# Two fold weights read in 4096-byte packets: whole rows of w3, pairs of rows of w_out, and a transpose by every second column

## The chip, the cores and the metric

The kernel runs on one core of one Trainium2 chip. The metric is the device time of one execution in microseconds (us); the time before is the median of three runs.

## The reference

Windowed attention with sink tokens, then a multiplicative feed-forward block:

```python
# q, k, v: (4, 8, 768, 64) float32; n_sink = 4, window = 128
scores = q @ k.T / sqrt(64), kept where key < 4 or 0 <= query - key < 128
x = (softmax(scores) @ v), heads side by side            # (3072, 512)
out = (((x @ w1) * (x @ w2)) @ w3) @ w_out               # w1, w2: 512x1024; w3: 1024x1024; w_out: 1024x512
```

All inputs and the output are float32; the kernel works in bfloat16.

## The kernel before

No activation stands between w3 and w_out, so the kernel first makes their product, the *fold* `w3o = w3 @ w_out` (1024 x 512, bfloat16), and then needs one projection for each token instead of two. For the fold, `fold_w3` (L398) transposes each block of 128 rows of w3 on TensorE, four 128 x 128 squares into a PSUM tile (L402), and VectorE copies them out (L407). `fold_mm` (L421) multiplies the eight transposed squares of row block `i` with the eight row blocks of w_out (L432), two at a time, and ScalarE copies the sum to `w3o` (L436, L439). Both weights lie in SBUF as bfloat16 (`w3_sb`, `wo_sb`), with a block of 128 rows for each index of the second dimension and one row in each partition.

The weights come in two ways. *Raw loads* (`load_raw`, L151) are issued by SP at the start: nine transfers of 512 KB of float32 into buffers that are only needed later (`homes`, L147), each then cast to bfloat16 by VectorE (w3) or ScalarE (w_out) (`cast`, L410). Each takes two row blocks, 512 columns wide. The rest of w3 comes through POOL's queue (`load_rows`, L114), which casts on the way, as do k, q and v (L106) and w1 and w2 (L110). The order of POOL's loads is the list `order` (L138), and POOL starts it only when the fifth raw load has landed (`hold`, L136, and the small copy at L195).

After the fold's first part the kernel goes through four batches: for each block of 256 tokens transposes of k and q (L205 on TensorE for the first two batches, by DMA for the others), scores and exponentials (L255, L276), masked, times v (L308, L345), a transpose of the result (L324, L361), then the two gate products with w1 and w2 (L385), their elementwise product, and the projection with `w3o` (L446) and the output's transfer (L453).

The engines' programs are written by hand-made planning at build time: every piece of work is a `task` (L513) with its stages, costs, predecessors and loads; `landings` (L475) forecasts when each load is there; from L724 on a loop always takes the task that can start first, with a priority among equals. The order that comes out is fixed in the program. Where the planner sees a gap on TensorE in the first 40 us, it puts in fillers, `keep_busy` (L456): products of a zero tile, whose result nobody reads. `need` (L524) tells the fold's tasks which cast or which load they wait for; the transposes of a w3 block need its columns, the products need w_out's blocks.

Of the kernel before, what the change touches and what calls it, by code (L numbers as in the profile page):

```python
# [21 lines left out]
def kernel(  # L22
# [13 lines left out]
    nc = tc.nc  # L36
    FP32 = mybir.dt.float32
# [7 lines left out]
    P = 128  # L45
# [3 lines left out]
    DM = H * D  # L49
# [61 lines left out]
        nc.gpsimd.dma_start(out=dst[:, :, n0:n1],  # L111
                            in_=src[:, n0:n1].rearrange("(ko ki) n -> ki ko n", ki=P))

    def load_rows(dst, src, i0, i1, cols):  # L114
        nc.gpsimd.dma_start(out=dst[:, i0:i1, cols],
                            in_=src[i0 * P:i1 * P, cols].rearrange("(ko ki) n -> ki ko n", ki=P))

    def load(what, *i):
        if what == "qkv":
            if i[1] == 0:  # L120
                nc.gpsimd.memset(vN[i[0]][:, :, :, D:D + 1], 1.0)
            for kb in range(i[1], i[2]):
                load_qkv(i[0], kb)
        elif what == "w3":
            load_rows(w3_sb, moe_w3, i[0], i[0] + 2, slice(i[1] * 512, i[2] * 512))
        elif what == "wo":
            load_rows(wo_sb, moe_w_out, i[0], i[1], slice(0, DM))
        else:
            for dst, src in ((w1_sb, moe_w1), (w2_sb, moe_w2)):
                load_w(dst, src, i[0] * 256, i[1] * 256)  # L130


    raws = [("w3", 0, 0, "dve"), ("wo", 0, 0, "act"), ("w3", 2, 0, "dve"), ("wo", 2, 0, "act"),
            ("w3", 4, 0, "dve"), ("wo", 4, 0, "act"), ("w3", 0, 1, "dve"), ("wo", 6, 0, "act"),
            ("w3", 2, 1, "dve")]
    hold = 5  # L136

    order = [("qkv", 0, 0, 1), ("w3", 4, 1, 2), ("qkv", 0, 1, 2), ("w3", 6, 0, 2), ("qkv", 0, 2, 3),  # L138
             ("qkv", 0, 3, 4), ("w12", 0, 1), ("w12", 1, 2), ("w12", 2, 3), ("w12", 3, 4), ("qkv", 0, 4, 5),
             ("qkv", 0, 5, 6), ("qkv", 1, 0, 6), ("qkv", 2, 0, 6), ("qkv", 3, 0, 6)]  # L140

# [2 lines left out]
    def flat(tile_, names):  # L144
        return tile_[:].rearrange(f"p {names} -> p ({names})")
# [2 lines left out]
    homes += [(flat(kN[1], "k s"), 0), (flat(qN[1], "k s"), 0), (flat(kqT[1], "i k s"), 0), (flat(kqT[1], "i k s"), 2048),  # L148
              (flat(xT[1], "k s"), 0), (flat(vN[2], "k h d"), 0)]

    def load_raw(n, what, i, h, act):  # L151
        home, at = homes[n]
        tile_ = home[:, at:at + 2048].bitcast(FP32).rearrange("p (k n) -> p k n", n=512)
        dst, src = (w3_sb, moe_w3) if what == "w3" else (wo_sb, moe_w_out)
        nc.sync.dma_start(out=tile_, in_=src[i * P:(i + 2) * P, h * 512:h * 512 + 512].rearrange(  # L155
            "(ko ki) n -> ki ko n", ki=P))
        return dst[:, i:i + 2, h * 512:h * 512 + 512], tile_

    ctx.enter_context(tc.manual_schedule(engines={
        mybir.EngineType.PE, mybir.EngineType.Activation, mybir.EngineType.DVE, mybir.EngineType.SP,  # L160
# [31 lines left out]
    for b in range(B):  # L192
        nc.gpsimd.tensor_copy(vs[b][:, :, D], ones_s[:])
    if hold:
        nc.gpsimd.tensor_copy(spent[:], casts[hold - 1][1][:, 0, 0:1])  # L195
    for x in order:
        if x[0] != "qkv" or x[1] == 0:
            load(*x)
# [199 lines left out]
    def fold_w3(i, j0, j1):  # L398

        tp = ps_mm.tile([P, j1 - j0, P], BF16, tag="mm", name="tp3")  # L400
        for j in range(j0, j1):
            nc.tensor.transpose(tp[:, j - j0, :], w3_sb[:, i, j * P:(j + 1) * P], ident)  # L402
        yield
        if i not in w3T:
            w3T[i] = (flat((kN, qN)[i - 4][1], "k s")[:, 2048:3072].rearrange("p (k n) -> p k n", n=P)
                      if i in (4, 5) else work.tile([P, KFF, P], BF16, tag="w3t", bufs=4, name="w3t"))
        nc.vector.tensor_copy(w3T[i][:, j0:j1, :], tp[:])  # L407
        yield

    def cast(act, dst, src):  # L410

        (nc.scalar.copy if act else nc.vector.tensor_copy)(dst, src)  # L412
        yield
# [51 lines left out]
    def service(what, *i):  # L465
        if what == "qkv":
            return [(0.95 if i[0] == 0 else 0.87, 0.845 + (1.2 if i[0] in XPOSE and x != "v" else 0.7 if (x, *i) == ("v", 0, 4, 5) else 0.0), [(x, i[0], kb)])
                    for kb in range(i[1], i[2]) for x in "kqv"]
        if what == "w3":
            return [(0.75, 1.3 * (i[2] - i[1]), [("w3", i[0], h) for h in range(i[1], i[2])])]  # L470
        if what == "wo":
            return [(0.81, 0.65 * (i[1] - i[0]), [("wo", x, 0) for x in range(i[0], i[1], 2)])]
# [46 lines left out]
    for n, ((what, i, h, e), ap) in enumerate(zip(raws, casts)):  # L519
        task(("c", what, i, h), n, cast(e == "act", *ap), [(e, 1.04 if e == "act" else 0.69)],  # L520
             loads=[("raw", what, i, h)])
    raw_keys = {x[:3] for x in raws}

    def need(what, i, h):  # L524
        key = (what, i // 2 * 2, h)
        return ([("c",) + key], []) if key in raw_keys else ([], [key])

    for i in range(KFF):
        for h in range(2):
            j0, j1 = 4 * h, 4 * h + 4  # L530
            needs = [need("w3", i, x) for x in range(j0 // 4, j1 // 4)]
            task(("t3", i, h), 100 + i + (5 if i < SPLIT and h else 0), fold_w3(i, j0, j1),
                 [("pe", 0.057 * (j1 - j0)), ("dve", 0.05 + 0.075 * (j1 - j0))],
                 [x for a, _ in needs for x in a], [x for _, a in needs for x in a],
                 started=[("t3", i, 0)] if i >= SPLIT and h else [folded(i - SPLIT)] if i >= SPLIT else [], ring="mm")
        for h, (j0, j1) in enumerate(FM[i]):
            last = j1 == KFF
            begin = i < 4 and i % 2 == 0 and h == 0
# [268 lines left out]
```

## Time and profile before

| | us |
|---|---|
| median of three runs | 198.62 (198.33 to 198.84) |
| profiled execution | 198.11 |
| its span | 196.40 |
| TensorE busy | 189.7 (97% of the span) |
| VectorE busy | 115.0 |
| ScalarE busy | 104.9 |
| GpSimd busy | 76.0 |

The profiled execution's time is 1.7 us longer than its span, which counts from the first to the last recorded instruction. In the rows, PE is TensorE's products, PEld its weight loads, DVE is VectorE, ACT ScalarE, POOL GpSimd, SP SyncE. A row of the timeline gives the start, the length from the first start to the last end, engine, line, operation, tiles and shapes, the number of instructions that follow each other, and in brackets the idle time of the engine ahead of them and what ended it. The names are those of the buffers: `w_sb` stands for all weight tiles, `ab`, `kN`, `qN` and `kqT` also for the buffers that a raw load borrows.

| queue | what | issues, KB each |
|---|---|---|
| SP | raw loads of w3 and w_out (L155) | 9, 512 |
| POOL | w1 and w2 (L111), a part of w3 (L115) | 9 of 256, 1 of 512 (as written) |
| POOL | k, q, v (L108) | 72, 128 (as written) |
| SP | output (L453) | 24 of 25 |

### The profile page before, as it was taken

Reading aid. Unit: us, or ns where it says so; the run is one execution under the profiler, and the core shown is the slowest. Engines: PE = TensorE matmul, PEld = TensorE weight load, DVE = VectorE, ACT = ScalarE, POOL = GpSimd, SP = SyncE. Lnnn points to the kernel's source line nnn. Section 1 sums busy time; section 2 is a strip of 40 time slices with the busy share of each in tenths; the row PEclk is TensorE's granted clock in tenths of the full one; section 3 lists DMA queues with packets and bytes.
Section 4 is the critical chain, followed back from the end, with each engine's and each line's share of the span. In section 5 each row is a group of like instructions: output and inputs, shape, how many; then the busy total and the mean of one; then the engine's idle time right before and its main releaser. Section 6 shows DMA issues by size and latency. Waiting matters only on the chain.

```text
span 196.4 us, 4491 instructions
## 1 busy us (share of the span) xinstructions
PE 189.7 (97%) x1778; PEld 119.2 (61%) x1792; DVE 115.0 (59%) x268; ACT 104.9 (53%) x174; POOL 76.0 (39%) x104
## 2 busy tenths in 40 slices
PE   7999889999999999999999999999999999999994
PEld 2345566988867687666666655666555556654443
DVE  4544778755767878687879738777644034440000
ACT  2334557744825788876777355556653433332332
POOL 5189967689999953745557000000000000000000
PEclk9999999999999999999999999999999999999999
DMA  5999999999999999999999999920232600002334
GB/s 145 390 389 189 184 158 197 196 162 154 156 152 212 187 183 125 153 162 177 158 151 159 121 156 178 97 57 2 53 110 107 180 35 3 0 0 96 143 140 158
DMA packets 105445, 28.35 MB, mean 144 GB/s; under 512 B 95184, under 2 KB 99920, under 8 KB 105424
## 3 DMA queue, kind: packets, MB, share of 16 engines
q0 software_dynamic: 79648, 12.33, 89.7%
q1 hardware_dynamic: 25632, 15.67, 35.7%
q8 instruction: 14, 0.23, 0.4%
q14 instruction: 7, 0.06, 0.1%
q10 hardware_dynamic: 144, 0.07, 0.1%
HBM read 29.36 MB, written 6.29 MB: 182 GB/s over the span
## 4 chain that ended last, share of the span: by engine, by line
PE 85%; DMA 8%; POOL 4%; SPq 1%; issue 1%; DVE 0%; ACT 0%
PE pg L385 43%; PE po L446 21%; PE av L345 7%; PE sc L255 5%; DMA ab<-in_moe_w_dram 4%; DMA w_sb<-in_moe_w_dram 4%; PE tp L205 3%; PE pw L432 2%; POOL qN L108 1%; PE xt L361 1%; POOL vN L108 1%; PE av L308 1%; SPq L155 1%; POOL kN L108 1%; PE sp L237 1%; PE sc L276 1%
## 5 line engine op out<-in xcount | busy, mean ns | idle before, releaser
L385 PE MATMUL pg<-xT,w_sb 128*128 128x384 bf16 (+1 forms) x576 | 90.8, 308 | 0.0
L385 PEld LDWEIGHTS <-w_sb 128*128 128x128 bf16 x576 | 53.5, 98 | 25.4 <-issue 0.5
L389 DVE TENSOR_TENSOR ab<-a_sb,pg 128x384 bf16<-128x384 f32 (+1 forms) x72 | 36.6, 508 | 29.1 <-PE pg L385 24.3
L392 ACT COPY a_sb<-pg 128x384 f32<-128x384 f32 (+1 forms) x72 | 32.0, 444 | 37.2 <-PE pg L385 17.8
L446 PE MATMUL po<-w3o,ab 128*128 128x512 bf16 (+2 forms) x198 | 42.6, 362 | 0.5
L260 ACT ACTIVATE ex<-sc 128x1024 bf16<-128x1024 f32 (+1 forms) x40 | 37.8, 964 | 5.0 <-PE sc L255 4.5
L446 PEld LDWEIGHTS <-ab 128*128 128x128 bf16 x208 | 19.3, 98 | 20.1 <-issue 0.3
L450 ACT COPY w_sb<-po 128x512 f32<-128x512 f32 (+2 forms) x25 | 14.1, 566 | 25.9 <-PE po L446 24.0
L264 DVE TENSOR_TENSOR am<-ex,maskt 128x1024 bf16<-128x1024 bf16 (+1 forms) x40 | 25.4, 645 | 4.0 <-ACT ex L260 4.0
L108 POOL DMA_DIRECT2D vN<-in_v_dram x24 | 21.9, 912 | 12.3 <-DMA kN<-in_k_dram 10.6
L108 POOL DMA_DIRECT2D qN<-in_q_dram x24 | 22.0, 917 | 5.9 <-DMA vN<-in_v_dram 3.8
L108 POOL DMA_DIRECT2D kN<-in_k_dram x24 | 21.7, 906 | 4.4 <-DMA qN<-in_q_dram 2.6
L352 DVE TENSOR_TENSOR xn<-av,rec 128x256 bf16<-128x256 f32 x40 | 17.0, 425 | 1.4
L345 PE MATMUL av<-vN,am 128*128 128x65 bf16 x296 | 16.4, 193 | 0.0
L345 PEld LDWEIGHTS <-am 128*128 128x128 bf16 x296 | 14.3, 97 | 2.4 <-issue 0.2
L349 DVE RECIPROCAL rec<-av 128x4 f32<-128x4 f32 x40 | 7.2, 179 | 11.0 <-PE av L345 10.7
L255 PE MATMUL sc<-kqT 64*128 64x128 bf16 (+1 forms) x216 | 11.6, 238 | 0.0
L345 PE MATMUL av<-vs,es 128*128 128x130 bf16 x56 | 11.0, 221 | 0.1
L207 DVE COPY kqT<-tp 128x1024 bf16<-128x1024 bf16 x12 | 8.3, 690 | 3.8 <-PE tp L205 3.6
L450 DVE COPY w_sb<-po 128x128 f32<-128x128 f32 x1 | 0.3, 292 | 16.3 <-ACT w_sb L450 16.3
L255 PEld LDWEIGHTS <-kqT 64*128 64x128 bf16 x216 | 6.9, 94 | 4.0 <-issue 3.2
L432 PE MATMUL ph<-wo_sb,w3t 128*128 128x512 bf16 x32 | 8.1, 379 | 0.5 <-ACT wo_sb L412 0.4
(71 smaller groups left out, 145.1 us busy)
## 6 DMA issues: line engine op xcount, KB each, us to landing
out_dram<-w_sb SPq DMA_DIRECT2D x23, 256.0 KB, 2.2
kN<-in_k_dram POOLq DMA_DIRECT2D x24, 128.0 KB, 8.0
qN<-in_q_dram POOLq DMA_DIRECT2D x24, 128.0 KB, 8.0
vN<-in_v_dram POOLq DMA_DIRECT2D x24, 128.0 KB, 7.8
w_sb<-in_moe_w_dram POOLq DMA_DIRECT2D x9, 256.0 KB, 8.4
ab<-in_moe_w_dram SPq DMA_DIRECT2D x3, 512.0 KB, 6.1
ab<-in_moe_w_out_dram SPq DMA_DIRECT2D x3, 512.0 KB, 7.0
kN<-in_moe_w_dram SPq DMA_DIRECT2D x1, 512.0 KB, 9.2
```

Of the source, the lines that this page charges most:

```text
L108: nc.gpsimd.dma_start(out=dst, in_=rows(src, b, kb))
L255: nc.tensor.matmul(sc[:, e, c:c + n], kT[b][hp, r, kb * P:(kb + 1) * P], qT[b][hp, r, qb * P:qb * P + n], start=True, stop=True)
L260: nc.scalar.activation(ex[:, :, c0:], sc[:, :, c0:], ACTF.Exp, scale=scale)
L264: nc.vector.tensor_mul(am[:, :, c0:], ex[:, :, c0:], mk)
L345: nc.tensor.matmul(o, lhs, rhs, start=(n == 0), stop=(n == len(todo) - 1), skip_group_check=True)
L352: nc.vector.tensor_mul(xns[b, t][:, :, r, :, :], av[:, :, :, 0:D], rec[:].to_broadcast([P, 2, 2, D]))
L385: nc.tensor.matmul(pg[:], w_sb[:, kk, dt * P:(dt + 1) * P], xT[b][:, kk, tk], start=(kk == 0), stop=(kk == NP - 1))
L389: nc.vector.tensor_mul(ab[b][:, dt, tk], gate_a.pop((b, c, dt))[:], pg[:])
L392: nc.scalar.copy(a_sb[:], pg[:])
L432: nc.tensor.matmul(po, w3T[i][:, j, :], wo_sb[:, j, :], start=(j == 0), stop=(j == KFF - 1))
L446: nc.tensor.matmul(po[:], ab[b][:, kk, m * P:(m + 1) * P], w3o[:, kk, n0:n1], start=(kk == 0), stop=(kk == KFF - 1))
L450: (nc.vector.tensor_copy if n0 == DM // 2 else nc.scalar.copy)(o_sb, po[:])
```

## The change

Raw loads and POOL's loads of w3 take whole rows: a raw load of w3 is now one block of 128 rows, 1024 columns wide, so that each partition reads 4096 adjacent bytes where it read two runs of 2048. A raw load of w_out takes 256 rows as before, but partition p gets rows 2p and 2p+1 of them, which lie next to each other, again 4096 bytes. So index j of `wo_sb` no longer holds rows 128j to 128j+127, but every second row of a group of 256. The transposes of w3 follow: square j takes every second column of w3, from j // 2 * 256 + j % 2, so that the products still pair the same rows and columns.

The raw loads' order changes with it: w_out's first 256 rows come first, then w3 and w_out in turn, and the ninth is w3's fifth block. POOL keeps one block of w3 (rows 640 to 767) as its first weight load, where it had the right halves of two blocks, and its last two blocks, which it read by whole rows already. The planner's tables follow the new units; its costs for a raw load, a cast and a transpose are the same numbers.

```diff
-    def load_rows(dst, src, i0, i1, cols):
-        nc.gpsimd.dma_start(out=dst[:, i0:i1, cols],
-                            in_=src[i0 * P:i1 * P, cols].rearrange("(ko ki) n -> ki ko n", ki=P))
+    def fold_rows(what, i0, i1):
+
+        src = (moe_w3 if what == "w3" else moe_w_out)[i0 * P:i1 * P, :]
+        if what == "w3":
+            return src.rearrange("(ko ki) n -> ki ko n", ki=P)
+        return src.rearrange("(g ki ko) n -> ki g (ko n)", ki=P, ko=2)
+
+    def load_rows(dst, what, i0, i1):
+        dst = dst[:, i0:i1, :]
+        if what == "wo":
+            dst = dst.rearrange("p (g ko) n -> p g (ko n)", ko=2)
+        nc.gpsimd.dma_start(out=dst, in_=fold_rows(what, i0, i1))
...
-    raws = [("w3", 0, 0, "dve"), ("wo", 0, 0, "act"), ("w3", 2, 0, "dve"), ("wo", 2, 0, "act"),
-            ("w3", 4, 0, "dve"), ("wo", 4, 0, "act"), ("w3", 0, 1, "dve"), ("wo", 6, 0, "act"),
-            ("w3", 2, 1, "dve")]
+    raws = [("wo", 0, 2, "act"), ("w3", 0, 1, "dve"), ("wo", 2, 4, "act"), ("w3", 1, 2, "dve"),
+            ("wo", 4, 6, "act"), ("w3", 2, 3, "dve"), ("wo", 6, 8, "act"), ("w3", 3, 4, "dve"), ("w3", 4, 5, "dve")]
     hold = 5
...
-    order = [("qkv", 0, 0, 1), ("w3", 4, 1, 2), ("qkv", 0, 1, 2), ("w3", 6, 0, 2), ("qkv", 0, 2, 3),
+    order = [("qkv", 0, 0, 1), ("w3", 5, 6), ("qkv", 0, 1, 2), ("w3", 6, 8), ("qkv", 0, 2, 3),
...
-    def load_raw(n, what, i, h, act):
+    def load_raw(n, what, i0, i1, act):
         home, at = homes[n]
-        tile_ = home[:, at:at + 2048].bitcast(FP32).rearrange("p (k n) -> p k n", n=512)
-        dst, src = (w3_sb, moe_w3) if what == "w3" else (wo_sb, moe_w_out)
-        nc.sync.dma_start(out=tile_, in_=src[i * P:(i + 2) * P, h * 512:h * 512 + 512].rearrange(
-            "(ko ki) n -> ki ko n", ki=P))
-        return dst[:, i:i + 2, h * 512:h * 512 + 512], tile_
+        tile_ = home[:, at:at + 2048].bitcast(FP32)
+        nc.sync.dma_start(out=tile_.rearrange("p (k n) -> p k n", k=1), in_=fold_rows(what, i0, i1))
+        return flat((w3_sb if what == "w3" else wo_sb)[:, i0:i1, :], "k n"), tile_
...
         for j in range(j0, j1):
-            nc.tensor.transpose(tp[:, j - j0, :], w3_sb[:, i, j * P:(j + 1) * P], ident)
+            nc.tensor.transpose(tp[:, j - j0, :], w3_sb[:, i, bass.ds(j // 2 * 256 + j % 2, P, step=2)], ident)
...
         if what == "w3":
-            return [(0.75, 1.3 * (i[2] - i[1]), [("w3", i[0], h) for h in range(i[1], i[2])])]
+            return [(0.75, 1.3 * (i[1] - i[0]), [("w3", x) for x in range(*i)])]
...
-            needs = [need("w3", i, x) for x in range(j0 // 4, j1 // 4)]
+            needs = [need("w3", i)]
...
-            needs = [need("wo", x, 0) for x in range(j0, j1, 2)]
+            needs = [need("wo", x) for x in range(j0, j1)]
```

In the built program TensorE's stream has the same work ahead of the transposes of k and q for the fifth token block of the first batch, and the same order from there on. Ahead of them 19 fillers stand instead of 16, and the fold's pieces stand in the new order of the loads.

More of the change, by code (lines that the diff above doesn't have):

```diff
@@ L124, in load @@
         elif what == "w3":
-            load_rows(w3_sb, moe_w3, i[0], i[0] + 2, slice(i[1] * 512, i[2] * 512))
+            load_rows(w3_sb, what, *i)
         elif what == "wo":
-            load_rows(wo_sb, moe_w_out, i[0], i[1], slice(0, DM))
+            load_rows(wo_sb, what, *i)
         else:
@@ L194 @@
     if hold:
-        nc.gpsimd.tensor_copy(spent[:], casts[hold - 1][1][:, 0, 0:1])
+        nc.gpsimd.tensor_copy(spent[:], casts[hold - 1][1][:, 0:1])
     for x in order:
@@ L469, in service @@
         if what == "w3":
-            return [(0.75, 1.3 * (i[2] - i[1]), [("w3", i[0], h) for h in range(i[1], i[2])])]
+            return [(0.75, 1.3 * (i[1] - i[0]), [("w3", x) for x in range(*i)])]
         if what == "wo":
-            return [(0.81, 0.65 * (i[1] - i[0]), [("wo", x, 0) for x in range(i[0], i[1], 2)])]
+            return [(0.81, 0.65 * (i[1] - i[0]), [("wo", x) for x in range(*i)])]
         return [(0.8, 1.34 * (i[1] - i[0]), [(w,) + (n,) for n in range(i[0], i[1])]) for w in ("w1", "w2")]
@@ L517, in task, with need @@
                            slots=slots, paced=paced)
[L519 to L526, printed above, removed]
+    made = {}
+    for n, ((what, i0, i1, e), ap) in enumerate(zip(raws, casts)):
+        task(("c", what, i0), n, cast(e == "act", *ap), [(e, 1.04 if e == "act" else 0.69)],
+             loads=[("raw", what, i0, i1)])
+        made.update({(what, i): ("c", what, i0) for i in range(i0, i1)})
+    def need(what, i):
+        return ([made[what, i]], []) if (what, i) in made else ([], [(what, i)])
     for i in range(KFF):
```

## Prediction

> **What bounds the kernel now.** I read the page first, then the chain of waits in order of time, then the timeline of the first 36 us, then the order of the instructions in both programs.
>
> ```profile
> span 196.4 us, 4491 instructions
> PE 189.7 (97%) x1778; PEld 119.2 (61%) x1792; DVE 115.0 (59%) x268; ACT 104.9 (53%) x174; POOL 76.0 (39%) x104
> PE 85%; DMA 8%; POOL 4%; SPq 1%; issue 1%; DVE 0%; ACT 0%
> ```
>
> TensorE has the end: 85% of the chain is its own. The next fences are the chain of waits in order of time (start, length, what) and the busy times by stretch (length, then each engine's busy time and instructions, for the first row TensorE's alone; then granted clock, DMA share, GB/s).
>
> ```profile
> 0.81 0.46 SPq L155
> ...
> 2.85 7.84 DMA ab<-in_moe_w_dram
> ...
> 10.74 0.71 POOL spent L195
> ...
> 11.69 0.81 POOL kN L108
> ...
> 18.32 7.46 DMA w_sb<-in_moe_w_dram
> ...
> 25.83 0.41 PE tp L402 x4
> ...
> 28.01 0.45 PE tp L205 x8
> 28.45 0.86 PE pw L432 x4
> ...
> 30.87 0.33 PE sc L276 x8
> ...
> 31.74 0.24 PE av L308 x8
> 31.99 0.22 PE sp L237 x4
> ...
> 33.73 0.36 PE av L308 x10
> ...
> 37.65 2.62 PE pg L385 x24
> ...
> 43.22 0.22 PE tp L205 x4
> ```
>
> ```profile
> 25.83:43.22 17.39, 17.17 (x221) 1.00 1.83 181
> ```
>
> ```profile
> 60.00:100.00 40.00, 39.84 (x476) 27.45 (x476) 31.17 (x80) 31.32 (x51) 25.01 (x30) 1.00 1.95 168
> 100.00:140.00 40.00, 39.95 (x399) 24.89 (x398) 28.99 (x68) 23.11 (x39) 4.37 (x5) 1.00 1.17 106
> ```
>
> The reader is to see two regimes. From 25.83 on TensorE is full, at a granted clock of 1.00, and sets its own pace. Before, the chain runs through transfers: the fifth raw transfer lands (2.85 + 7.84 = 10.69), POOL starts its loads, and the last w3 rows land at 25.78. So time is to be had only where TensorE stands without useful work ahead of some 28 us. The order view says that both programs' TensorE streams are the same from the transposes at 43.22 on, and that ahead of them they hold the same work but for 19 fillers instead of 16. So the change is worth the difference in idle and filler time up to that mark, and that difference stays to the end.
>
> By the chain's rows, a transpose takes 0.45/8 = 0.056 us, a fold product 0.86/4 = 0.215, a gate product of 256 columns 2.62/24 = 0.109. Up to the mark the order view counts 64 fold products (13.8), 112 transposes (6.3) and 64 gate products (7.0) in both programs, seven groups of scores at 0.33 (2.3), three and four groups of values at 0.24 and 0.36 (2.2), and two sink steps, each taken at 0.22 (0.4): 32.0 us of work. Before stands **43.22 - 32.0 = 11.2 us without work**.
>
> **The change part by part.** The timeline's rows for the start (start, length, engine, line, tile):
>
> ```profile
> 1.33 4.87 PE L460 MATMUL pz<-ksbd 128*128 128x512 bf16 x11 [1.33 <-DVE ksbd L165]
> ...
> 5.32 0.79 DVE L412 CAST w_sb<-ab 128x1024 bf16<-128x1024 f32 x1 [1.73 <-DMA ab<-in_moe_w_dram]
> ...
> 6.17 0.78 PE L402 MATMUL tp<-ident,w_sb 128*128 128x128 bf16 x8
> 6.67 1.04 ACT L412 CAST wo_sb<-ab 128x1024 bf16<-128x1024 f32 x1 [4.59 <-DMA ab<-in_moe_w_out_dram]
> ...
> 8.00 0.69 DVE L412 CAST w_sb<-ab 128x1024 bf16<-128x1024 f32 x1 [0.47 <-DMA ab<-in_moe_w_dram]
> ...
> 8.75 0.62 PE L402 MATMUL tp<-ident,w_sb 128*128 128x128 bf16 x8
> ...
> 9.35 1.04 ACT L412 CAST wo_sb<-ab 128x1024 bf16<-128x1024 f32 x1 [1.63 <-DMA ab<-in_moe_w_out_dram]
> ...
> 9.67 2.76 PE L432 MATMUL ph<-wo_sb,w3t 128*128 128x512 bf16 x12
> ...
> 25.00 0.39 PE L460 MATMUL pz<-ksbd 128*128 128x512 bf16 x1
> 25.83 0.40 PE L402 MATMUL tp<-ident,w_sb 128*128 128x128 bf16 x4 [0.45 <-DMA w_sb<-in_moe_w_dram]
> ```
>
> *Raw transfers.* Each moves 512 KB before and after; the casts show one landing every (9.35 - 5.32)/3 = 1.34 us. What changes is 128 packets of 4096 bytes for 256 of 2048. No HWDGE packet of 4096 bytes reading HBM is in this trace. The nearest rows are the raws themselves (queue totals of 6 to 14 us) and the POOL load of the last w3 rows, which already reads whole rows (22.5 to 23.5 us; packets counted at the 2048 bytes written, so twice that is read):
>
> ```profile
> DMA packets 1620, 3.12 MB, mean 390 GB/s; under 512 B 96, under 2 KB 96, under 8 KB 1620
> q1 hardware_dynamic: 1620, 3.12, 104.8%
> ```
>
> ```profile
> q0 software_dynamic: 97, 0.20, 104.9%
> ```
>
> At the same share of the engines 390 GB/s stand against 97 x 4096 bytes in 1 us, 397, or 400 by the rounded megabytes. Bounds: no gain (1.34 us a raw), and a tenth (1.21), which no row here reaches. I take 1.29, a little over the nearest row, as its packets are also cast: 0.05 us a raw, 0.2 at the fourth landing, 0.45 at the ninth.
>
> The Trainium skill (DMA: Bandwidth & Descriptors, "Why small descriptors are slow (HBM only)") gives each packet about 3 cycles on top of its 32-byte beats; as an estimate from that page 3/67 at 2048 bytes becomes 3/131 at 4096, 2.2% saved, a raw of 1.31 and a sum 0.2 us poorer than below (nine raws at 0.02 ahead of the last load). The POOL row's 2% agrees with it.
>
> *Order of the raws and start of the fold.* w_out comes first, so the first w3 rows are the second landing: 6.67 - 0.1 = 6.57, cast 0.79, hop 0.06 (8.00 + 0.69 to 8.75), transposes at 7.4, where 6.17 stood before. The four added fillers cover it: ten spacings in 4.87 less a last one of 0.57 are 0.43 each, so twelve to fifteen end between 7.3 and 7.8, and either hides in the next wait. The second w3 block needs the fourth landing: 9.35 - 0.2 + 0.69 + 0.06 = **9.90**. TensorE has done eight transposes and four products by then (1.3 us), since only w_out's first blocks are there: 8.6 without work. The gap between transposes and their products (copy by DVE) is 9.67 - 8.75 - 0.45 = 0.47; the new order has it twice more (it puts one filler in each): 9.5. From about 15 us on, all of w_out and four w3 blocks are there and the order finds work for every copy.
>
> *The last loads.* POOL's hold is on the fifth landing, 0.25 earlier; its first load was issued at 11.69, yet between 6 and 14 us the raws' queue alone moved (the only queue row above), so I let its stream begin as the raws end, 0.45 earlier; the load of w3 rows 640 to 767 has 128 packets instead of 256. The last w3 rows land some 0.5 earlier, 25.3. Counted as above, 15.4 us of work stand ahead of their transposes before (so 25.83 - 15.4 = 10.4 without work there); the new order has the same work and four more transposes there, 15.6. TensorE comes to them at 15.6 + 9.5 = 25.1 and the load ends at 25.3: the filler and most of the wait of 25.00 to 25.83 go, and 25.3 - 15.6 = 9.7 are without work. After that, before loses another 11.2 - 10.4 = 0.8; the new order puts twelve transposes in a row ahead of one pair of products, so I add a half gap, 0.25. **After: 9.7 + 1.05 = 10.75 without work, 0.5 less than before.**
>
> *Transposes by every second column.* 64 weight loads now read w3_sb with a step of two elements.
>
> ```profile
> L402 PEld LDWEIGHTS <-w_sb x64: 95/98/152, 6.2 to 27.3; 128*128 128x128 bf16 x64
> ```
>
> ```profile
> 79.24 0.71 PE av L345 x20
> ```
>
> Twenty matmuls with a load each take 0.71, so a load with adjacent elements holds TensorE at most 36 ns, though its record lasts 98. A transpose takes 56. No load with a step is in this trace: its cost is bounded by 0 (it hides under the 56) and by the whole record exposed, 98 - 56 = 42 ns. I take 0, by the 20 ns of slack of the nearest row.
>
> The Trainium skill (TensorE: Matmul & The Clock Gate, "Weight-path perf modes — Fast Weight Load (FWL) and DoubleRow") speaks against this: the fast load reads 32 bits at a time, two bf16, and a step of two leaves one of use. As an estimate a load would then hold 72 ns, 16 more than a transpose, 0.8 us for the 48 transposes that don't stand in a wait, and the sum would be +0.3. The same table allows a step, and no run here shows one.
>
> *Nothing* I count for the rest: five casts of 0.69 on DVE, four of 1.04 on ACT, sixteen copies of 0.42 and nine SP issues stay, and POOL's order is the same. The products pair w3 and w_out rows of the same index, so their sum is unchanged.
>
> **Sum:** 196.4 - 0.5 = 195.9 of span. The profiled execution took 198.11, 1.7 over its span: 197.6. It lies 0.5 under the median of 198.62, so on that scale 198.1.
>
> **The rivals.**
>
> *The step costs (slower).* The loads stand in front of every transpose; the first 16 fall into waits for landings, 48 are on the path after 10 us. At 42 ns each 2.0 us go, with -0.5 that is +1.5: **200.1**. From 10 ns a transpose on (66 ns instead of 56) the gain is gone; from 23 ns on the kernel is slower by over 0.3%. For it: no such load is known here. Against: the 20 ns of slack.
>
> *The ramp shrinks too (faster).* The first landing comes at 5.32, 4.5 us after its issue at 0.81, against 1.34 between the later ones. If a part of that start goes by packet, half as many packets bring every landing some 0.5 more forward, the POOL stream with them: **197.6**. Against: bytes may set it, not packets.
>
> *The last load holds.* If POOL's stream doesn't come forward, the last w3 rows still land at 25.78 and TensorE waits for them from 25.1 on; 25.8 - 15.6 + 1.05 = 11.25 without work: **198.6**, no change. For it: the chain passes through this very load; in POOL's order six loads of k, q and v stand ahead of it, which the change leaves alone.
>
> *The new order meets waits that the planner does not see.* It still plans 1.31 us a raw and the old price of a transpose; three more gaps of 0.47 between copies and products in 15 to 25 us, where I count none, cost 1.4: **199.5**.
>
> **How the numbers follow.** The forecast, 197.6 to 198.6, has 0.46; its middle lies close to what a measurement of this kernel can just tell from no change, 0.3% or 0.6 us, so I split it 0.23 faster, 0.23 same. The ramp 0.15 (faster), the last load 0.10 (same), the step 0.23 (slower), new waits 0.06 (slower). Faster 0.38, same 0.33, slower 0.29. The range goes from 197.2, beyond the ramp's case by what a raw of 1.21 would add in the first four landings, to 200.1, which takes in a step at 42 ns.
>
> **What would show it.** Casts about 1.29 apart (a raw's gain right) or 1.34 (wrong); eight transposes of L402's successor in 0.45 (no cost of the step) or 0.6 and more; first transposes at 7.4, second block at 9.9; no wait of a transpose on a w_sb load at 25 to 26 us; the transposes of 43.22 at about 42.7. If these stand at 43.2 or later while the casts came closer, the time went to waits between 10 and 28 us; if the stream after the mark is longer, my claim that the difference stays is wrong.

## The result, and the profile after

The kernel after takes **197.92 us** (median of 22 runs, 196.73 to 198.6), the kernel before 198.53 on the same chip (22 runs, 198.06 to 199.82). The ratio is 0.996, with a 95% interval from 0.9946 to 0.9975: 0.6 us or 0.4% faster. The profiled execution took 197.96 us, 1.7 over its span.

The page, head and chain by engine:

```profile
span 196.3 us, 4494 instructions
PE 188.9 (96%) x1781; PEld 118.8 (61%) x1795; DVE 114.6 (58%) x268; ACT 105.2 (54%) x174; POOL 75.4 (38%) x104
PE 86%; DMA 7%; DVE 3%; issue 1%; ACT 1%; SPq 1%; POOL 0%
```

The span is 0.1 shorter than that of before, although the median fell by 0.6; the profiled execution of before (198.11) lies 0.4 under its own median, that of after at its median. So the two spans are not the gain; the places where the streams part are what the traces can show.

The timeline of the start (casts, then TensorE's transposes of the first two w3 blocks):

```profile
4.19 1.04 ACT L418 CAST wo_sb<-ab 128x1024 bf16<-128x1024 f32 x1 [2.10 <-DMA ab<-in_moe_w_out_dram]
5.43 0.69 DVE L418 CAST w_sb<-ab 128x1024 bf16<-128x1024 f32 x1 [1.84 <-DMA ab<-in_moe_w_dram]
7.53 1.04 ACT L418 CAST wo_sb<-ab 128x1024 bf16<-128x1024 f32 x1 [2.29 <-DMA ab<-in_moe_w_out_dram]
8.80 0.69 DVE L418 CAST w_sb<-ab 128x1024 bf16<-128x1024 f32 x1 [1.42 <-DMA ab<-in_moe_w_dram]
10.09 1.04 ACT L418 CAST wo_sb<-ab 128x1024 bf16<-128x1024 f32 x1 [1.51 <-DMA ab<-in_moe_w_out_dram]
11.37 0.70 DVE L418 CAST w_sb<-ab 128x1024 bf16<-128x1024 f32 x1 [0.63 <-DMA ab<-in_moe_w_dram]
...
6.19 0.62 PE L408 MATMUL tp<-ident,w_sb 128*128 128x128 bf16 x8
...
8.63 0.59 PE L438 MATMUL ph<-wo_sb,w3t 128*128 128x512 bf16 x2 [0.92 <-ACT wo_sb L418]
...
9.55 0.62 PE L408 MATMUL tp<-ident,w_sb 128*128 128x128 bf16 x8
```

From the third landing on a raw transfer lands every (11.37 - 7.53)/3 = 1.28 us, where it was 1.35. The first landing comes 1.1 us earlier than before, but between the second and the third lie 2.1 us, so that the fourth is only 0.55 ahead (8.80 for 9.35). The queue totals between 6 and 14 us agree in direction, 401 GB/s for 390:

```profile
DMA packets 1103, 3.21 MB, mean 401 GB/s; under 512 B 327, under 2 KB 327, under 8 KB 1103
q1 hardware_dynamic: 883, 3.18, 98.9%
```

The chain of waits in order of time shows what replaced the w3 load that held TensorE at 25.78:

```profile
2.20 6.58 DMA ab<-in_moe_w_dram
8.80 0.70 DVE w_sb L418
9.55 0.41 PE tp L408 x4
...
42.50 0.45 PE tp L211 x8
...
52.41 6.92 DMA qN<-in_q_dram
59.38 0.40 PE tp L211 x4
```

It now leaves the transfers at the fourth raw landing, 2.20 + 6.58 = 8.78, and passes no load from there to the mark. The mark, 43.22 before, stands at **42.50: 0.72 us earlier**. But at 52 us the chain goes back to a transfer, q of the second batch's fifth token block (of six). The waits of TensorE on other engines and queues between 6 and 70 us (total, times, longest):

```profile
PE ph L438 <- ACT wo_sb L418: 0.9, 1, 0.9
PE pw L438 <- DVE w3t L413: 0.4, 1, 0.4
PE tp L211 <- DMA qN<-in_q_dram: 0.4, 1, 0.4
PE ph L438 <- DVE w3t L413: 0.3, 1, 0.3
```

No wait of a product on w_sb is left in this list, though the second block's transposes still start when their cast ends (8.80 + 0.69 = 9.49); the filler ahead of them covers most of that wait. The third row is the new one; its place in the timeline, and the same transposes in the kernel before:

```profile
58.60 0.40 PE L211 MATMUL tp<-ident,kN 128*128 128x128 bf16 x4
59.38 0.40 PE L211 MATMUL tp<-ident,qN 128*128 128x128 bf16 x4 [0.38 <-DMA qN<-in_q_dram]
```

```profile
59.18 0.38 PE L205 MATMUL tp<-ident,kN 128*128 128x128 bf16 x4
59.53 0.40 PE L205 MATMUL tp<-ident,qN 128*128 128x128 bf16 x4
```

Laid instruction by instruction over that of before, TensorE's stream is 0.89 ahead at 43.4, 0.84 at 49.8, and 0.15 from 59.5 to the last product. In this execution, then, most of what the fold gained went back to POOL's stream of k, q and v. The landings in the two traces show how: from the second batch's first load to v of its third block POOL's loads land 0.7 to 0.8 us earlier than before, nearly as much as TensorE had gained. The next load, k of the fourth block, follows 1.72 us behind that v, where it was 1.15, and from there the stream is less than 0.3 ahead: the q that TensorE waits for lands at 59.33, before at 59.48.

### The profile page after: what moved, and what is told of

The parts are those of the page before. It is cut to its first block, busy times and chain, and to the rows that moved or that the text cites. A ratio compares the mean times of both kernels' runs of the same rounds, so it can differ in the third digit from the quotient of the medians.

```text
span 196.3 us, 4494 instructions
## 1 busy us (share of the span) xinstructions
PE 188.9 (96%) x1781; PEld 118.8 (61%) x1795; DVE 114.6 (58%) x268; ACT 105.2 (54%) x174; POOL 75.4 (38%) x104
## 4 chain that ended last, share of the span: by engine, by line
PE 86%; DMA 7%; DVE 3%; issue 1%; ACT 1%; SPq 1%; POOL 0%
PE pg L391 41%; PE po L452 19%; PE av L351 6%; PE sc L261 5%; DMA qN<-in_q_dram 4%; PE pw L438 3%; DMA ab<-in_moe_w_dram 3%; PE ph L438 3%; PE tp L211 2%; PE tp L408 1%; PE av L314 1%; PE xt L367 1%; PE sc L282 1%; DVE w3t L413 1%; PE sp L243 1%
## 5 line engine op out<-in xcount | busy, mean ns | idle before, releaser
L438 PE MATMUL ph<-wo_sb,w3t 128*128 128x512 bf16 x32 | 8.6, 380 | 1.4 <-ACT wo_sb L418 0.9
```

The lines of the kernel that those rows point to most:

```text
L438: nc.tensor.matmul(po, w3T[i][:, j, :], wo_sb[:, j, :], start=(j == 0), stop=(j == KFF - 1))
```

## The experiments

They ran in four groups, the first two on one chip and the last two on another, each beside the kernels of its group and runs of the kernel before (median 198.69, 199.0, 198.44 and 198.43 in the four). Times are medians, and ratios, to the kernel before of the same group, have their 95% interval behind them.

**Order alone: the packets of 2048 bytes again.** POOL's loads of w3 by whole rows stay as in the kernel after; no run parts them from the order.

```diff
-        nc.sync.dma_start(out=tile_.rearrange("p (k n) -> p k n", k=1), in_=fold_rows(what, i0, i1))
+        if what == "w3":
+            src = moe_w3[i0 // 2 * 256:i0 // 2 * 256 + 256, i0 % 2 * 512:i0 % 2 * 512 + 512]
+        else:
+            src = moe_w_out[i0 * P:i1 * P, :]
+        nc.sync.dma_start(out=tile_.rearrange("p (k n) -> p k n", n=512),
+                          in_=src.rearrange("(ko ki) n -> ki ko n", ki=P))
```

> The changed kernel, but each raw load reads the same bytes in 256 packets of 2048, as before: two row blocks by 512 columns of w3, two rows 128 apart of w_out. Order, sizes, step of the transposes and TensorE's stream stay; the fold pairs wrong rows, so the output is not the reference's. Theory (the packets bring the raws forward): landings again at 5.3 and every 1.34 us, second w3 block's transposes at 10.1 instead of 9.55, the mark (transposes of k and q for the fifth token block) at 43.0 to 43.3 instead of 42.5, time within 0.3 us of the kernel before. Rival (the new order of loads and products does it): landings late, but the mark at 42.5 to 42.7 and the changed kernel's time.

198.57 us, 0.9991 (0.9973 to 1.0009): no gain. The casts stand at 4.29, 6.85, 8.58 and 9.94, then 1.35 apart as before, and TensorE's transposes of the second w3 block wait for the fourth of them (timeline, TensorE):

```profile
9.68 0.59 PE L443 MATMUL ph<-wo_sb,w3t 128*128 128x512 bf16 x2 [0.55 <-ACT wo_sb L423]
10.11 0.38 PE L471 MATMUL pz<-ksbd 128*128 128x512 bf16 x1
10.69 0.62 PE L413 MATMUL tp<-ident,w_sb 128*128 128x128 bf16 x8 [0.20 <-DVE w_sb L423]
```

They start at 10.69, 1.1 later than in the kernel after, and the transposes of k for the fifth token block stand at 43.70, later than in the kernel before (the profiled execution was the longest of its runs, 198.97). The new order needs the landings early: it has less to do than the old one until the second block is there. Its first landing at 4.29 also shows that the early start does not come from the larger packets alone.

**Packets alone: the old order and tiling with raw transfers of 4096 bytes.**

```diff
-        nc.sync.dma_start(out=tile_, in_=src[i * P:(i + 2) * P, h * 512:h * 512 + 512].rearrange(
-            "(ko ki) n -> ki ko n", ki=P))
+        rows_ = (src[(i + h) * P:(i + h + 1) * P, :].rearrange("(ko ki) n -> ki ko n", ki=P) if what == "w3" else
+                 src[i * P:(i + 2) * P, :].rearrange("(g ki ko) n -> ki g (ko n)", ki=P, ko=2))
+        nc.sync.dma_start(out=home[:, at:at + 2048].bitcast(FP32).rearrange("p (k n) -> p k n", k=1), in_=rows_)
```

> The kernel before, with its order and its transposes of adjacent columns, but each raw load reads 512 KB in 128 packets of 4096; the rows that land are not those that the fold takes them for, so the output is not the reference's. Theory (packets): first landing at 4.2 instead of 5.3, first transposes at 5.0 to 5.1, landings every 1.28, the last w3 load from POOL 0.7 earlier, mark 0.6 to 0.8 earlier than 43.2, time 0.4 to 0.7 us under the kernel before. Rival (order): mark at 43.0 or later and the time of the kernel before.

198.36 us, 0.9996 (0.9968 to 1.0024). The profiled execution was the longest of its runs (200.13): TensorE waited 2.0 us for the last w3 rows there. So it was run again in the second group:

> The kernel before with packets of 4096 bytes for the raw loads and its own order and tiling of the fold (rows and columns paired wrongly, same amount of work), once more, since the profile of the first time fell on its longest run. Theory (with the old order the 0.06 us of each raw transfer end at the last w3 rows through POOL): raw casts 1.28 apart, the transposes at the end of the fold wait 0.5 us or more for the last w3 rows at 25 to 27 us, and the transposes of the fifth token block stand within 0.4 us of 43.2. Rival (the packets alone bring the gain, and the first profile was only an outlier): no such wait, those transposes at 42.7 or earlier, and 0.5 us or more under the kernel before.

198.63 us, 0.9979 (0.9959 to 1.0). From the third to the eighth the casts are 1.28 apart (once 1.35), and the longest waits of TensorE between 6 and 70 us are these, with the place of the second in the timeline:

```profile
PE tp L403 <- DVE w_sb L413: 1.2, 1, 1.2
PE tp L403 <- DMA w_sb<-in_moe_w_dram: 1.0, 1, 1.0
PE pw L433 <- DVE kN L408: 0.8, 2, 0.5
PE tp L206 <- DMA qN<-in_q_dram: 0.5, 1, 0.5
```

```profile
24.61 0.39 PE L461 MATMUL pz<-ksbd 128*128 128x512 bf16 x1
26.04 0.40 PE L403 MATMUL tp<-ident,w_sb 128*128 128x128 bf16 x4 [1.05 <-DMA w_sb<-in_moe_w_dram]
```

TensorE comes to these transposes earlier than in the kernel before and waits 1.05 instead of 0.45, as the load itself lands no earlier (26.00 for 25.79); the transposes of k for the fifth token block stand at 43.20 (43.05 before). This is the rival "the last load holds", in the old order. By medians the packets alone are worth 0.3 to 0.4 us, and the intervals reach or touch no change; the order alone is worth nothing that its interval shows; both together gave 0.6 us in the result and 0.85 and 0.73 in the second and third group. In the second group the intervals of the packets alone and of both overlap, so that the order adds to the packets is shown by the marks (43.20 and, in the first run, 44.36, against 42.2 to 42.9 in the table below) more than by the times.

**The step taken away, and made larger.** The first leaves the transposes on adjacent columns, the second reads every eighth.

```diff
-            nc.tensor.transpose(tp[:, j - j0, :], w3_sb[:, i, bass.ds(j // 2 * 256 + j % 2, P, step=2)], ident)
+            nc.tensor.transpose(tp[:, j - j0, :], w3_sb[:, i, j * P:(j + 1) * P], ident)
...
+            nc.tensor.transpose(tp[:, j - j0, :], w3_sb[:, i, bass.ds(j, P, step=8)], ident)
```

> The changed kernel with the transposes of w3 reading adjacent columns instead of every second one, so that the fold pairs wrong columns; nothing else differs. Theory (the step costs nothing): eight transposes in 0.45 in both, mark within 0.1 us of the changed kernel's, time within 0.3. Rival (a part of the step's cost is hidden in the gain): mark 0.3 to 1.0 earlier, time as much less.

> The kernel after with the 64 transposes of w3 reading every eighth column (a step of 16 bytes) instead of every second (4 bytes); rows and columns are then paired wrongly, so the fold's result differs, the work's amount does not. Theory (a weight load's step costs nothing as such): eight transposes in 0.45 us and records of 96 to 100 ns as before, time that of the kernel after. Rival (a step costs by the width that is read, and two elements were still within it): a transpose takes over 70 ns, eight over 0.55, and the 48 transposes off the waits add 0.7 us or more at the mark.

Without the step: 197.5 us, 0.9945 (0.9924 to 0.9965), not apart from the kernel after (0.996 in the result; it did not run in this group). With a step of eight: 197.71, 0.9922 (0.9892 to 0.9952), beside 198.15 for the kernel after in its group, so its time shows no cost either. Its trace does. The transposes' weight loads (count, then min/median/max in ns) in the kernel after and with the step of eight, each with the twelve transposes in a row at the end of the fold:

```profile
L408 PEld LDWEIGHTS <-w_sb x64: 96/98/100, 6.2 to 27.0; 128*128 128x128 bf16 x64
...
25.22 0.83 PE L408 MATMUL tp<-ident,w_sb 128*128 128x128 bf16 x12
```

```profile
L408 PEld LDWEIGHTS <-w_sb x64: 142/146/170, 6.5 to 27.7; 128*128 128x128 bf16 x64
...
25.90 0.90 PE L408 MATMUL tp<-ident,w_sb 128*128 128x128 bf16 x12
```

A step of two costs nothing: 98 ns, as for adjacent elements, where the twelve transposes take 0.83 us too. A step of eight makes the load's record 48 ns longer, and twelve transposes take 0.07 us more, 6 ns each: most of the longer load still hides under the transposes. That theory, that a step costs nothing as such, falls for a step of 16 bytes; the rival's 0.7 us at the mark did not come either, it was 0.2 (table below).

**What sets the mark: the second w3 block.** In the profiles with the new order and the large packets the transposes of k for the fifth token block follow the first transposes of the second w3 block at one distance (starts by the timelines):

```profile
43.05 0.39 PE L205 MATMUL tp<-ident,kN 128*128 128x128 bf16 x4
```

```profile
42.34 0.39 PE L211 MATMUL tp<-ident,kN 128*128 128x128 bf16 x4
```

The first row is the kernel before, the second the kernel after.

| kernel | second block | k, fifth token block | between |
|---|---|---|---|
| after | 9.55 | 42.34 | 32.79 |
| after, second group | 10.13 | 42.91 | 32.78 |
| after, third group | 10.02 | 42.80 | 32.78 |
| adjacent columns | 9.44 | 42.23 | 32.79 |
| k and q first | 9.46 | 42.26 | 32.80 |
| last block's k and q first | 9.89 | 42.66 | 32.77 |
| step of eight | 10.05 | 43.04 | 32.99 |
| before | 8.75 | 43.05 | 34.30 |
| old order, large packets (again) | 8.73 | 43.20 | 34.47 |

The new order takes 1.5 us out of this stretch and gives back 0.7 to 1.4 by starting it later. How much is left differs from run to run with the fourth landing. The last w3 load through POOL is no bound in the profiles with the new order: it lands 0.2 to 1.1 us before TensorE comes to its transposes. The rows are those of k; q of the same block comes through POOL too, and in seven of the nine it holds the transposes behind k by another 0.1 to 0.6 us. To test what sets the mark, the fourth landing was brought forward: the second w3 block cut to its left half.

```diff
+        n1 = 512 if n == 3 else 1024
-        nc.sync.dma_start(out=tile_.rearrange("p (k n) -> p k n", k=1), in_=fold_rows(what, i0, i1))
+        nc.sync.dma_start(out=tile_[:, 0:n1].rearrange("p (k n) -> p k n", k=1),
+                          in_=fold_rows(what, i0, i1)[:, :, 0:n1])
...
+    nc.gpsimd.memset(casts[3][1][:, 512:1024], 0.0)
```

> The kernel after with the fourth raw load (w3's second block) cut to its left 512 columns, 128 packets of 2048 bytes; the right half of its buffer is zeroed by POOL ahead of time, so the fold's second block of rows is not the reference's, with the same work and order on TensorE. That landing and all raw landings behind it, the fifth that starts POOL's queue too, then come some 0.64 us earlier. Theory (in the new order nothing stands still on TensorE between the second block's transposes and the mark, so the mark is that start plus 32.9 us, and 42.5 to 43.0 in the profiles of the kernel after because that start lies between 9.4 and 10.1): the second block's transposes start 0.5 to 0.7 earlier for a given third landing, the transposes of k and q for the fifth token block stand 32.9 us behind them within 0.2, without a wait for w_sb at 25 us, and the median lies 0.3 to 0.7 us further under the kernel before than the kernel after's 0.6 to 0.85. Rival (the last w3 rows or q of the fifth token block through POOL are close behind and hold the mark): those transposes stand 33.3 us or more behind the second block's, with a wait of TensorE on w_sb or qN ahead of them, and the median is that of the kernel after.

**197.26 us**, 0.9926 (0.9903 to 0.995), 1.17 under the kernel before. Rows of TensorE's timeline, the second block's transposes with the two rows ahead of them, and the transposes of k:

```profile
9.34 0.59 PE L441 MATMUL ph<-wo_sb,w3t 128*128 128x512 bf16 x2 [1.21 <-ACT wo_sb L421]
9.77 0.38 PE L469 MATMUL pz<-ksbd 128*128 128x512 bf16 x1
9.98 0.61 PE L411 MATMUL tp<-ident,w_sb 128*128 128x128 bf16 x8
...
42.67 0.39 PE L214 MATMUL tp<-ident,kN 128*128 128x128 bf16 x4
```

42.67 - 9.98 = 32.69, with no wait on w_sb or qN ahead of it: the theory's distance. The start itself is no earlier than in the table, as the third landing was late in this execution (8.24; it was the longest of its runs, 197.69) and the fourth came 0.97 us behind it. So the profile doesn't show the gain; the median does: it lies 0.3 to 0.55 further under the kernel before than the kernel after's did, with ratios whose intervals overlap (on the same chip its nine runs took 196.74 to 197.69, the twelve of the kernel after in the third group 196.85 to 198.51). The rows show the next bound, which I had not seen: the two products ahead wait for the cast of the third landing (w_out's rows), and with the filler behind them they end at 9.98 just as the fourth landing's cast (9.21 + 0.69) is done. In the profile after the same two products, at 8.63, and their filler end some 0.27 us before the transposes start at 9.55. So, as an estimate from these rows, bringing the fourth landing forward pays for some 0.3 us, and then the third one holds.

**What gives the gain back.** First all pairs of the second batch's loads were put in the order k, q, k, q, v, v, then only the last pair:

```diff
...
+            if i[0] == 1:
+                for kb in range(i[1], i[2], 2):
+                    load_qkv(1, kb, (0, 1))
+                    load_qkv(1, kb + 1, (0, 1))
+                    load_qkv(1, kb, (2,))
+                    load_qkv(1, kb + 1, (2,))
+                return
```

> The changed kernel, but POOL issues the second batch's loads by pairs of token blocks: k, q, k, q, v, v instead of k, q, v, k, q, v. TensorE's stream is the same and the output is the reference's. Theory (after the mark the k and q loads of the second batch's last token block hold TensorE and take back 0.7 of the 0.9 us gained): these loads land one v load, 0.85 us, earlier, the wait of 0.2 + 0.6 us at 58.4 to 59.4 goes, the gain at the mark stays to the end: time 0.5 to 0.8 us under the changed kernel. Rival (the wait is an accident of the one profiled run, or the v loads hold instead): time of the changed kernel within 0.3 us, or a wait on v at the same place.

199.13 us, 1.0031 (1.0007 to 1.0055): slower than before. The wait at 59 us is gone, and a longer one stands at 50, on v of the first block (waits of TensorE):

```profile
PE vp L240 <- DMA vN<-in_v_dram: 1.5, 1, 1.5
```

That v had gone from the third place of the batch's loads to the fifth. The q that the kernel after waits for at 59.38 is the fifth block's, and not the last one's as the expectations say; it is the fourteenth of the batch's loads in the kernel after, here and in the next run alike. So neither run moves the load that held. Here it lands at 58.43, and TensorE, after the wait on v, comes to it only at 60 us.

> The kernel after, with one change: of the second batch's loads by POOL only those of the last two token blocks change places, k, q, k, q, v, v instead of k, q, v, k, q, v. So v of the first blocks, which the run with all pairs changed had to wait for at 50 us, stays in its place. Theory (the gain at the mark is handed back at 58 to 59 us, where the transposes wait for k and q of the last token block): these land about 0.85 us earlier, one load's time at POOL's pace, the wait of the transposes on them (0.67 in the kernel after's profile) is gone, and the median lies 0.2 to 0.7 us under that of the kernel after in the same call. Rival (the wait only moves: to v of the last two blocks, which now land 0.85 later, or to a later transfer): a wait of a product on vN stands at 60 to 66 us and the median is that of the kernel after to 0.2 us or longer.

> The kernel after itself, unchanged, beside the others of this call. Theory: 0.3 to 0.9 us under the kernel before, with a spread of its runs over 1 us, since the last part of the gain hangs on when k and q of the last token block land; the profiled run shows the transposes of k and q for the fifth token block at 42.3 to 42.8 and a wait of 0 to 0.7 us for the second batch's last block, and its time follows from that wait. Rival (the gain is spread over the run and not kept or lost at that one place): the end's gain differs from the mark's without such a wait.

The last of these is the kernel after, unchanged; the one before it changes this:

```diff
...
+            if i[0] == 1:
+                for kb in range(4):
+                    load_qkv(1, kb)
+                for kb, which in ((4, (0, 1)), (5, (0, 1)), (4, (2,)), (5, (2,))):
+                    load_qkv(1, kb, which)
+                return
```

With only the last pair changed 197.95 us, 0.9935 (0.9915 to 0.9956), beside 198.15, 0.9952 (0.9922 to 0.9981), for the kernel after in the same group: 0.2 by medians, and not apart. The two profiles lose time to POOL's stream in smaller pieces at 46 and 50 us, and the one with the last pair changed another 0.66 us at 101, most of it a wait of 0.5 of scores for a transpose of q by DMA. The kernel after this time waits by its weight loads on q of the first batch's last block and v of the second batch's first, and not at 59 us (waits of TensorE's weight loads, 42 to 64 us):

```profile
PEld L261 <- issue: 0.4, 2, 0.2
PEld L232 <- DMA vN<-in_v_dram: 0.3, 1, 0.3
PEld L211 <- DMA qN<-in_q_dram: 0.2, 1, 0.2
```

So the hold is not one transfer but the whole stream: whichever of its loads TensorE comes to with no slack. In the three profiles of the kernel after POOL's loads mostly land 0.8 to 0.9 us apart between 42 and 60 us, with a pause of 1.6 to 1.7 somewhere: at 54 to 56 us in the first, 44 to 46 in the second, 42 to 43.6 in the third (which has one of 1.5 at 55 too). The longer waits come at its end or behind it. In the third group POOL's queue was made lighter, in both kernels (the values then use `vhead`, the head modulo four); the third kernel of the group is the kernel after, unchanged:

```diff
...
+            part = slice(0, H // 2) if b == 1 and kb > 0 and src is v else slice(0, H)
-            nc.gpsimd.dma_start(out=dst, in_=rows(src, b, kb))
+            nc.gpsimd.dma_start(out=dst[:, part, :], in_=rows(src, b, kb)[:, part, :])
...
```

The cut starts with v of the second block, which lands at 51 us, so it lightens nothing ahead of that: holds at 43 to 50 us are outside it.

> The kernel after, with less in POOL's queue: of the second batch's v only the first four heads are loaded for token blocks 1 to 5 (of 128), and the values of heads 4 to 7 use those of heads 0 to 3; the output of that batch is not the reference's, TensorE's work and every engine's order are unchanged. Five loads of some 0.95 us become half as long, so k and q of the second batch's last block land up to 1.9 us earlier. Theory (the gain at the mark is handed back at 46 to 60 us because TensorE then keeps step with POOL's stream of k, q and v): no wait of TensorE on kN, qN at 56 to 60 us, the lead that the stream has at 52 us is still there or larger at the end, and the median lies 0.3 to 0.8 us under that of the kernel after in this call. Rival (the lead is lost by something else, or the spread of the runs comes from the start alone): median within 0.2 us of the kernel after's, and the same spread of its runs.

> The kernel before with the same cut: half of the second batch's v for token blocks 1 to 5, values of heads 4 to 7 from heads 0 to 3. Theory: the kernel before arrives at these transposes late enough that POOL's stream holds it little, so it gains less than the kernel after does, 0 to 0.4 us; without the hold the two kernels then differ by 0.7 to 1.1 us. Rival (both meet the same hold): it gains as much as the kernel after does and the difference stays at 0.6.

> The kernel after, unchanged, for comparison in this call: 0.3 to 0.9 us under the kernel before by either theory.

The kernel after with half of v: 197.64 us, 0.9962 (0.9935 to 0.9989); unchanged: 197.71, 0.9943 (0.9915 to 0.9971); before with half of v: 198.63, 1.0003 (0.998 to 1.0027). **My theory missed here.** The trace does what it said: the q at 59 us lands at 57.39, and no wait of TensorE on POOL's stream is left in this profile:

```profile
PE ph L442 <- ACT wo_sb L422: 0.9, 1, 0.9
PE pw L442 <- DVE w3t L417: 0.4, 1, 0.4
```

But the median fell by 0.07 and not by 0.3 to 0.8. The three profiles of the unchanged kernel after lose 0.3 to 0.6 us against that of before between the mark's transposes of k and 60 us, and the medians do not show that taking this away is worth as much. The test is a weak one: part of that is lost ahead of the cut, and before with half of v still waits 0.3 us for v of the first block at 50. With the lighter queue the medians of the two kernels differ by 1.0 us, without by 0.73, but the ratios say the opposite (0.4% and 0.6%; one run with the lighter queue took 200.92), so not even the direction is shown. The run-to-run spread, 1.7 us for the kernel after in this group (196.85 to 198.51), did not shrink either. The second half of the mechanism, that POOL's stream hands back part of the gain, is shown in profiles and not in medians; its size stays open within some 0.5 us. The profiles can't give the net gain either: that of before is of a run below its median (198.11), and those of the kernel after in the second and third group (198.29 and 198.51, both over their medians) end 0.2 and 0.4 us behind it, while the medians lie 0.85 and 0.73 under.

## Why the prediction was right

The forecast was 198.1 us, 0.5 under before; measured are 0.6, 0.85 and 0.73 us under. By its own steps:

- *Raw transfers, 1.29 us each:* 1.28 measured. The choice "a little over the nearest row" was right; the 3 cycles a packet of the Trainium skill (DMA: Bandwidth & Descriptors, "Why small descriptors are slow (HBM only)"; 1.31) were too little. In the traces the median packet of the raw transfers takes 159 ns for 4096 bytes and 84 for 2048, so two of the small ones cost 5.7% more, where that rule gives 2.3%.
- *First transposes 7.4, second block 9.9:* they started at 6.19 and 9.55 in the profile after, and at 9.44 to 10.13 over the others. The second block, which matters, was met; the first did not matter, as forecast. The landings before it went another way than in the forecast: the first two over 1 us earlier, the third 1.9 to 2.6 us behind the second. The two misses cancel, so that 9.9 was met is partly luck. The fillers' sum was off too: at 0.43 each, twelve to fifteen would end between 6.6 and 7.9, and the fifteen in the profile after took 4.83 us in all; nothing hung on it.
- *Last loads, 25.3, no wait of 0.45 left:* the twelve transposes start at 25.22 with no wait in front of them. The load landed at 24.31 in the profile after and at 24.7 to 25.6 in the others with the new order and large packets, always before TensorE came to it. The ledger let the load hold by 0.2 us (25.1 and 25.3); it does not hold, and TensorE's own stretch behind the second block is the bound.
- *The mark, 43.22 - 0.5 = 42.7:* 42.50, and some 0.5 later in the other two profiles of the kernel after. From the second block's transposes to the mark the ledger had 42.7 - 9.9 = 32.8 us; the profile after has 42.50 - 9.55 = 32.95 by the same rows, and six of the table's seven rows with the new order have one and the same distance to 0.03. This is the step that carried the prediction: it counted the work and the three gaps of copies, and nothing else was there.
- *The step, 0 ns:* right. The 32-bit rule of the Trainium skill (TensorE: Matmul & The Clock Gate, "Weight-path perf modes — Fast Weight Load (FWL) and DoubleRow") would have put the mark 0.8 us later, and the trace disagrees for a step of two elements: 98 ns a load and 0.83 us for twelve transposes. A step of eight does cost, but 6 ns a transpose.
- *"That difference stays to the end":* wrong as a claim. In the profile after, 0.84 us of lead became 0.15 at 59.4, where TensorE waits for q of the second batch through POOL's queue. The prediction named the ledger up to the mark as the whole matter and left out that the loads at and behind the mark come through a queue with no slack: TensorE then goes by their landings (59.33 for 59.48 before), whatever it gained ahead of them. The forecast of the time was met all the same, with medians 0.6 to 0.85 us under; the profiles don't show how much the hold counts in the median, so this part of the hit may be luck.

The stretches of 60 to 100 and 100 to 140 us, where the stream is unchanged, bear out the rest (length, then TensorE's busy time):

```profile
60.00:100.00 40.00, 39.84 (x473) 27.35 (x473) 30.86 (x79) 31.43 (x51) 23.11 (x29) 1.00 2.03 161
100.00:140.00 40.00, 39.95 (x399) 24.87 (x398) 29.04 (x68) 23.17 (x39) 6.06 (x7) 1.00 1.24 109
```

TensorE's 39.84 and 39.95 are those of before.

Of the rivals, *the step costs* and *new waits* fell. *The ramp shrinks too* was half there: the first landing came 1.1 us earlier, but small packets gave 4.29 as well, and the third landing was back where the forecast had it. *The last load holds* is what the packets alone run into with the old order (a wait of 1.05 us); the new order took that wait away.

## What to carry to other kernels

When a hand-made order removes the last wait in a stretch, the stretch becomes a constant behind its first input: measure that distance (here 32.8 us) over a few profiles, and look for the time in the landing that starts it. Larger packets and a new order can each be worth next to nothing and still pay together, because one brings data earlier and the other lets TensorE use it. A gain ahead of a full load queue is safe only as far as the loads behind it have slack: look at the first wait after it, not only at the place that was changed.

## What the runs showed of the hardware

The start of the transfers is uneven. In the trace of after, the packets of the raw transfers from 2 to 6 us have single ones of up to 525 ns among a median of 159; from 6 to 9 us none takes over 253. Each transfer ends with sixteen small writes, as many as the core has DMA engines, and the cast starts after the last: in the profile after, thirteen of the third raw transfer's stand between 5.98 and 6.36 us and three between 7.03 and 7.17, and each of the next five transfers has three that are some 0.7 us behind the others too. A part that was late once stays late, so the third landing comes 2.1 us behind the second, and all later ones keep the loss. As these packets differ from profile to profile, they may be why the runs spread; that, and what slows them, is open.

The first landing stands at 4.0 to 4.3 us where it is rows of w_out or whole rows of w3, and at 5.3 and 5.4 in the two profiles where it is half rows of w3 (before, and before with half of v). With the small packets in the new order the first landing, rows of w_out, stands at 4.29 and the second, half rows of w3, at 6.85; before it is the other way round, 5.32 and 6.67; with whole rows the second stands at 5.4 to 5.7. So in these profiles the loss goes with half rows of w3 among the first two transfers. No run tells whether the address pattern or something else makes this 1.1 us.

What makes the pauses in POOL's stream is open as well. In the profile after a packet of 16 KB on an instruction queue (q8) starts at 52.8 us and takes 1.47 us, just ahead of the pause at 54 to 56, and one stands within some 2 us of each pause named above. But other profiles have such packets at the same place and no pause (old order with large packets, 43.2 and 52.7), so that these are the cause is not shown.
